# T5-bias attention and a mixture of adapters: tail bias in PSUM, a single value tile, work per pair, and a new head and close

## The chip, the cores and the metric

One core of a Trainium2 chip. The metric is the device time of one execution in microseconds. TensorE (PE) multiplies matrices into PSUM (8 banks), VectorE (DVE) and ScalarE (ACT) read PSUM, GpSimd (POOL) works on SBUF only, SyncE (SP) issues most DMAs. Each engine runs its instructions in program order and waits on semaphores for the others.

## The reference

Attention over 8 batches, 8 heads, 576 positions of 64, with a bias that depends on the distance of two positions (constant from distance 128 on), then for each of the 4608 rows a mixture of two out of eight adapters of rank 16:

```python
scores = scale * np.matmul(q, k.transpose(0, 1, 3, 2)) + bias
attn = np.exp(scores - max); attn = attn / (sum(attn) + 1e-09)
x = matmul(attn, v)                      # to (B * S, H * D)
logits = x @ w_gate                      # 8 experts, the two largest kept
w = softmax over the two
delta = sum over the two of w * ((x @ A[e]) @ B[e])
return x + delta
```

All inputs and the output are fp32.

## The kernel before

The kernel works on pairs of heads: 4 pairs a batch, 32 pairs. Of the 576 positions, 512 are split into four tiles (g = 0 to 3), and the last 64 of both heads share one 128-row tile, the tail (g = 4). A pair so has five slots; in each, `qk` multiplies scores into `sc` (two buffers of two PSUM banks), `expo` (L349) turns them into probabilities `p` in bf16, and `band` multiplies those near the diagonal by the exponential of the bias: tables M for g < 4, M4 for the tail's rows and columns, MHT for tail by tail (`tail_scores`, `tail_band`). Far from the diagonal the bias is constant and drops out in the division.

`transposes` brings q and k of a pair to kqT through PSUM (`kqps`), `tail_transposes` does so for a batch's tails (`tps` to `tlT`). `pv` multiplies probabilities with the values of `vn` and of the tail `vt`, each with a column of ones that gives the sum; 41 matmuls a pair go into two PSUM tiles of three and two row blocks. `recip` and `norm` then divide, once for each tile, into `x`; `mask_tail` zeroes the tail's off-diagonal halves. The mixture of a batch follows in later pairs: `m_xdma` transposes x by DMA (the last two batches by TensorE, `m_x`), `m_logits`, `m_gate`, `m_z`, `m_zT`, `m_out`; the tails of two batches are joined through the selecting matrix `sel` in `m_xtail` and `m_outt`.

k, q and v come as fp32 on SP's queue and are cast to bf16 by GpSimd; the tails come through GpSimd's converting DMAs (`load_tail`, L133). One bank-sized pool `acc` of four buffers serves kqps, tps, pv and all of the mixture.

The order on each engine is that of the program: one loop over 160 slots (`n = 5 * i + g`) calls `qk(n + 1)`, `expo(n)`, and then the other steps at slots that are written out. Every DVE instruction is recorded through a helper and so has line 82.

Of the kernel before, what the change touches and what calls it, by code (L numbers as in the profile page):

```python
# [27 lines left out]
def kernel(  # L28
# [13 lines left out]

    nc = tc.nc
# [10 lines left out]
    MW = 384  # L54
    PSUM = bass.MemoryType.PSUM
# [6 lines left out]
    pp = ctx.enter_context(tc.tile_pool(name="probs", bufs=2))  # L62
    xp = ctx.enter_context(tc.tile_pool(name="x", bufs=2))
    sp = ctx.enter_context(tc.tile_pool(name="small", bufs=3))
    op = ctx.enter_context(tc.tile_pool(name="outs", bufs=3))
    scp = ctx.enter_context(tc.tile_pool(name="sc_ps", bufs=2, space=PSUM))
    acp = ctx.enter_context(tc.tile_pool(name="acc_ps", bufs=4, space=PSUM))

    ident = cp.tile([128, 128], BF16, tag="ident")
    make_identity(nc, ident)  # L70
# [23 lines left out]


    kfs, vns, vfs = {}, [], {}

    def alloc_loads(b):
        kf = ldp.tile([128, H, 4 * D], FP32, name="kf", tag="kf")
        qf = ldp.tile([128, H, 4 * D], FP32, name="qf", tag="qf")  # L100
        kfs[b] = (kf, qf)
        vfs[b] = ldp.tile([128, 4, H, D], FP32, name="vf", tag="vf")

    def load_kq(b, h0, h1):
        for t, src in zip(kfs[b], (k, q)):
            nc.sync.dma_start(
                out=t[:, h0:h1, :],
                in_=src[b, h0:h1, :S4, :].rearrange("h (p j) d -> p h (j d)", j=4))

    def load_v(b, js, eng=None):  # L110
        vr = v[b, :, :S4, :].rearrange("h (t p j) d -> j t p h d", t=4, j=4)
        for j in js:
            for t in range(4):
                (eng or nc.sync).dma_start(out=vfs[b][j * 32:(j + 1) * 32, t, :, :],
                                           in_=vr[j, t])

    tls, vts = [], []
    for i in range(2):  # L120
        tl = cp.tile([128, 2, HP, 128], BF16, name=f"tl{i}", tag=f"tl{i}")
        tls.append(tl)
        vt = cp.tile([128, HP, 2 * D1], BF16, name=f"vt{i}", tag=f"vt{i}")
        vts.append(vt)
        vn = cp.tile([128, 4, H, D1], BF16, name=f"vn{i}", tag=f"vn{i}")
        vns.append(vn)

    def load_tail(b, w, e):
        sr = (k, q, v)[w][b, :, S4:, :].rearrange("(c e) p d -> e p c d", e=2)
        s = slice(e * 64, (e + 1) * 64)  # L130
        o = (tls[b % 2][s, w, :, s] if w < 2 else
             vts[b % 2][s, :, e * D1:e * D1 + D])
        nc.gpsimd.dma_start(out=o, in_=sr[e])  # L133
# [3 lines left out]
    def cast_kq(i, w, eng=None):  # L137
        b, hp = divmod(i, HP)
        if w == 0:
            kqn[i] = knp.tile([128, 2, 4, 2, D], BF16, name="kqn", tag="kqn")  # L140
        o = kqn[i][:, w].rearrange("p j h d -> p h j d")
        s = kfs[b][w][:, 2 * hp:2 * hp + 2, :].rearrange("p h (j d) -> p h j d", j=4)
        if eng is nc.scalar:
            for h in range(2):
                nc.scalar.copy(o[:, h], s[:, h])
        else:
            return (eng or nc.gpsimd).tensor_copy(o, s)  # L147

    def cast_v(i, eng=None):
        b, hp = divmod(i, HP)  # L150
        h = slice(2 * hp, 2 * hp + 2)
        return (eng or nc.gpsimd).tensor_copy(vns[b % 2][:, :, h, :D],  # L152
                                              vfs[b][:, :, h, :])

    alloc_loads(0)
    btT = cp.tile([H, NB], FP32, tag="btT")
    nc.sync.dma_start(out=btT, in_=bias_table.rearrange("b h -> h b"))
    load_kq(0, 0, 2)
    for t in tls[:1] + vts[:1]:
        dve.memset(t, 0.0)  # L160
    dve.memset(vns[0][:, :, :, D:D1], 1.0)
    for w in range(2):
        for e in range(2):
            load_tail(0, w, e)
    load_v(0, (0, 1))
    load_kq(0, 2, 4)
    load_v(0, (2, 3))
    load_kq(0, 4, 6)


# [22 lines left out]
    for bv, lo, hi in runs[nsm:]:  # L193
        n = hi - lo
# [4 lines left out]
    ge = cp.tile([H, 512], BF16, tag="ge")  # L199
    nc.scalar.activation(ge, g_sb, ACT.Exp)  # L200
    g_d = nc.dram_tensor("g_d", (H, 512), BF16, kind="Internal")
    nc.scalar.dma_start(out=g_d.ap(), in_=ge)
    cast_kq(0, 0, dve)
    cast_kq(0, 1, dve)
    cast_kq(1, 0, dve)
    cast_kq(1, 1, dve)
    gt = g_d.ap()

    Mr = cp.tile([128, H, MW], BF16, tag="Mr")
    MHr = cp.tile([128, HP, 192], BF16, tag="MHr")  # L210
    for h0, h1 in ((0, 2), (2, 4), (4, H)):
        for j in range(4):
            nc.sync.dma_start(
                out=Mr[j * 32:(j + 1) * 32, h0:h1, :],
                in_=bass.AP(tensor=gt.tensor, offset=gt.offset + h0 * 512 + j,
                            ap=[[4, 32], [512, h1 - h0], [1, MW]]))
        if h0 == 0:
            for e in range(2):
                nc.sync.dma_start(
                    out=MHr[e * 64:(e + 1) * 64],  # L220
                    in_=bass.AP(tensor=gt.tensor, offset=gt.offset + e * 512 + 192,
                                ap=[[1, 64], [1024, HP], [1, 192]]))
        if h0 == 2:
            load_kq(0, 6, H)

    M = cp.tile([128, H, 4, 96], BF16, tag="M")
    M4 = cp.tile([128, HP, 256], BF16, tag="M4")
    MHT = cp.tile([128, HP, 2, 64], BF16, tag="MHT")  # L230

    def at(t, off, *dims):
        return bass.AP(tensor=t.tensor, offset=t.offset + off,
                       ap=[t.ap[0]] + [list(d) for d in dims])

    def bias_pair(hp, eng):
        eng.tensor_copy(M[:, 2 * hp:2 * hp + 2],
                        at(Mr, 2 * hp * MW + MW - 1, (MW, 2), (-1, 4), (-4, 96)))
        eng.tensor_copy(
            M4[:, hp, 0:128].rearrange("p (j u) -> p j u", j=4),  # L240
            at(MHr, hp * 192 + 191, (-1, 4), (-4, 32)))
        eng.tensor_copy(
            M4[:, hp, 128:256].rearrange("p (h t) -> p h t", h=2),
            at(Mr, 2 * hp * MW + 127, (MW, 2), (-1, 64)))
        if hp == 0:
            eng.tensor_copy(MHT, at(MHr, 63, (192, HP), (0, 2), (-1, 64)))

    load_tail(0, 2, 0)
    load_tail(0, 2, 1)
    for t in tls[1:] + vts[1:]:  # L250
        nc.gpsimd.memset(t, 0.0)
    for vt in vts:
        nc.gpsimd.memset(vt[0:64, :, D:D1], 1.0)
        nc.gpsimd.memset(vt[64:128, :, 2 * D + 1:2 * D1], 1.0)
# [3 lines left out]
    mask = cp.tile([128, 2, 2], FP32, tag="mask")  # L258
    nc.gpsimd.memset(mask, 1.0)
    nc.gpsimd.memset(mask[64:128, 1, 0:1], 0.0)  # L260
    nc.gpsimd.memset(mask[0:64, 1, 1:2], 0.0)


    sel = cp.tile([128, 2, 128], BF16, tag="sel")
    nc.gpsimd.memset(sel, 0.0)
    for e in range(2):
        for hf in range(2):
            s = slice(hf * 64, (hf + 1) * 64)
            nc.gpsimd.tensor_copy(sel[s, e, e * 64:(e + 1) * 64], ident[s, s])

# [4 lines left out]
    def load_weights(c):  # L275
        if c < 4:
            nc.gpsimd.dma_start(out=Ab[:, c].rearrange("p (e r) -> p e r", e=E),
                                in_=moe_A[:, c * 128:(c + 1) * 128, :]
                                .rearrange("e d r -> d e r"))
            return  # L280
        nc.gpsimd.dma_start(out=Wb,
                            in_=moe_w_gate.rearrange("(c p) e -> p c e", p=128))
        nc.gpsimd.dma_start(out=Bb, in_=moe_B.rearrange("e r d -> (e r) d"))


    kqT, tlT, scs, probs, ptl, xs = {}, {}, {}, {}, {}, {}
    TPOS = {3: 0, 0: 1, 1: 2, 2: 3}

    def transposes(i):
        n = kqn.pop(i)  # L290
        ps = acp.tile([128, 2, S4], BF16, name="kqps", tag="acc")
        for w in range(2):
            for j in range(4):
                o = (ps[:, 0].rearrange("p (t j u) -> p t j u", t=4, j=4)[:, :, j] if w == 0 else
                     ps[:, 1, j * 128:(j + 1) * 128])
                nc.tensor.transpose(o, n[:, w, j], ident)  # L296
        t = kqp.tile([128, 2, S4], BF16, name="kqT", tag="kqT")
# [12 lines left out]
    def tail_scores(b):  # L310
        t = tlT[b]
        ps = acp.tile([128, HP, 128], FP32, name="tsc", tag="acc")
        for c in range(HP):
            nc.tensor.matmul(ps[:, c, :], lhsT=t[:, 0, c, :], rhs=t[:, 1, c, :],
                             start=True, stop=True)
        p = pp.tile([128, HP, 128], BF16, name="ptl", tag="ptl")
        nc.scalar.activation(p, ps, ACT.Exp, scale=scale)
        ptl[b] = p

    def tail_band(b):  # L320
        p = ptl[b]
        dve.tensor_tensor(p, p, MHT.rearrange("p c e t -> p c (e t)"), op=ALU.mult)

    def qk(n):
        i, g = divmod(n, 5)
# [4 lines left out]
        if g < 4:  # L330
            for h in range(2):
# [6 lines left out]
        nc.tensor.matmul(sc[:, 0:512], lhsT=tt[:, 0, hp, :], rhs=t[:, 1, :],  # L338
                         start=True, stop=True)
        for j in range(4):  # L340
            o = 512 + TPOS[j] * 128
            nc.tensor.matmul(sc[:, o:o + 128], lhsT=t[:, 0, j * 128:(j + 1) * 128],  # L342
                             rhs=tt[:, 1, hp, :], start=True, stop=True,
                             skip_group_check=True)

    def expo(n):
        i, g = divmod(n, 5)
        p = pp.tile([128, 2 * S4], BF16, name=f"p{g}", tag=f"p{g}")
        nc.scalar.activation(p, scs.pop(n), ACT.Exp, scale=scale)  # L349
        probs[(i, g)] = p  # L350

    def band(n):
        i, g = divmod(n, 5)
# [343 lines left out]
```

## Time and profile before

| | |
|---|---|
| median of 3 runs | 229.74 us (228.09, 229.74, 230.37) |
| span of the profiled execution, first to last instruction | 227.5 us; its own time is one of such runs, 0.6 to 2.9 us above the span |
| first, last of the 160 exponentials start | 13.26, 205.1 us |
| an exponential (128 x 1024) | 1.03 us, one starts 0.90 us after the other when nothing is waited for |
| GpSimd's tail DMAs | 48, 0.61 to 0.64 us of GpSimd each, 4.2 to 6.2 us to landing |
| kf, qf of a batch (1 MB each) | 6.2, 12.2 us to landing |
| DMA moved | 41.01 MB, 180 GB/s |

A page's busy share is a mean over stages; the windows give it by stage. In a row of a group, the number after the busy time is the mean duration in ns. Times in the chain of waits are start and length. Neighbouring instructions of one engine overlap, so that steps from start to start are shorter than durations.

### The profile page before, as it was taken

The page shows a single profiled execution, that of the slowest core. Times are in us where ns is not written, and L with a number is a line of the kernel's source. Part 1 is how long each engine was busy: PE and PEld are TensorE (multiplying, and loading weights), DVE is VectorE, ACT ScalarE, POOL GpSimd, SP SyncE. Part 2 cuts the span into 40 slices and gives each one's busy share as a digit, 9 for nine tenths or more (in the row PEclk, how much of TensorE's full clock was granted, in tenths as well). Part 3 has the DMA queues.
Part 4 walks back from the last instruction along what each step waited for, and adds up shares of the span by engine and source line. Part 5 has one row for each costly group of instructions (what it writes and reads, how often), then busy time and mean ns, then how long its engine had stood idle before and what let it go on. Part 6 is the DMA issues. An engine that isn't in the chain of part 4 may idle for free.

```text
span 227.5 us, 6531 instructions
## 1 busy us (share of the span) xinstructions
PE 176.7 (78%) x2501; PEld 120.0 (53%) x2512; DVE 188.7 (83%) x571; ACT 160.0 (70%) x178; POOL 101.5 (45%) x191
## 2 busy tenths in 40 slices
PE   0174942988989998897899689898996999977651
PEld 0032622665665665665666457566663767655520
DVE  7046881889998999998999798999996989999862
ACT  3057570899999987996889588998894788792000
POOL 8530393755554546453555445555553442220000
PEclk9998595899999999999999999999999799999958
DMA  6986899899989999999179999998699720222406
GB/s 134 205 183 189 264 237 116 155 276 131 171 253 250 146 233 278 206 92 247 76 194 300 179 247 321 160 174 217 168 311 162 188 96 0 95 95 49 184 0 230
DMA packets 86935, 41.01 MB, mean 180 GB/s; under 512 B 66800, under 2 KB 84344, under 8 KB 86904
## 3 DMA queue, kind: packets, MB, share of 16 engines
q1 hardware_dynamic: 69000, 38.75, 70.0%
q0 software_dynamic: 17888, 1.85, 17.6%
q8 instruction: 19, 0.31, 0.6%
q14 instruction: 12, 0.10, 0.2%
q10 hardware_dynamic: 16, 0.01, 0.0%
HBM read 29.84 MB, written 9.45 MB: 173 GB/s over the span
## 4 chain that ended last, share of the span: by engine, by line
DVE 35%; PE 31%; DMA 17%; ACT 8%; issue 4%; SPq 2%; POOL 1%; POOLq 0%; ACTq 0%; DVEq 0%
DMA tl<-in_q_dram 11%; DVE p L82 11%; PE pv L382 9%; ACT p L349 8%; PE sc L333 7%; DVE x L82 5%; DVE o L82 4%; PE kqps L296 3%; DVE kqT L82 3%; DVE rc L82 2%; DMA qf<-in_q_dram 2%; PE sc L338 2%; PE zp L513 2%; PE sc L342 2%; DMA g_d<-ge 2%
## 5 line engine op out<-in xcount | busy, mean ns | idle before, releaser
L349 ACT ACTIVATE p<-sc 128x1024 bf16<-128x1024 f32 x160 | 153.3, 1034 | 33.2 <-PE sc L333 14.1
L82 DVE TENSOR_TENSOR p<-p,M 128x512 bf16<-128x512 bf16 (+2 forms) x192 | 76.3, 423 | 0.0
L333 PE MATMUL sc<-kqT 64*128 64x512 bf16 x256 | 51.6, 403 | 17.3 <-ACT p L349 8.7
L382 PE MATMUL pv<-vn,p 128*128 128x65 bf16 (+1 forms) x1152 | 61.6, 200 | 0.0
L382 PEld LDWEIGHTS <-p 128*128 128x128 bf16 x1280 | 52.5, 100 | 11.7 <-issue 10.4
L147 POOL CAST kqn<-qf 128x512 bf16<-128x512 f32 x29 | 18.0, 620 | 38.8 <-DVE rc L82 38.7
L152 POOL CAST vn<-vf 128x512 bf16<-128x512 f32 x28 | 17.3, 619 | 29.9 <-DVE p L82 21.4
L333 PEld LDWEIGHTS <-kqT 64*128 64x128 bf16 x256 | 13.5, 94 | 32.4 <-issue 18.1
L382 PE MATMUL pv<-vt,p 128*128 128x130 bf16 x128 | 28.6, 223 | 0.0
L296 PE MATMUL kqps<-ident,kqn 128*128 128x128 bf16 x256 | 21.3, 229 | 8.9 <-DVE kqn L82 8.1
L296 PEld LDWEIGHTS <-kqn 128*128 128x128 bf16 x256 | 15.3, 102 | 17.8 <-DVE kqn L82 8.4
L82 DVE COPY kqT<-kqps 128x1024 bf16<-128x1024 bf16 x32 | 21.8, 682 | 2.2 <-PE kqps L296 2.1
L82 DVE TENSOR_TENSOR o<-dl,x 128x512 f32<-128x512 f32 x32 | 21.4, 680 | 0.9 <-PE dl L534 0.9
L147 POOL CAST kqn<-kf 128x512 bf16<-128x512 f32 x29 | 17.8, 614 | 9.5 <-DVE p L82 6.6
L82 DVE TENSOR_TENSOR x<-pv,rc 128x384 bf16<-128x384 f32 x32 | 17.8, 557 | 1.3 <-DVE rc L82 0.2
L82 DVE RECIPROCAL rc<-pv 128x6 f32<-128x6 f32 x64 | 11.7, 183 | 5.4 <-PE pv L382 5.1
L305 PE MATMUL tps<-ident,tl 128*128 128x128 bf16 x64 | 6.4, 236 | 11.3 <-DMA tl<-in_q_dram 11.3
L342 PEld LDWEIGHTS <-kqT 128*128 128x128 bf16 x128 | 10.6, 104 | 8.1 <-issue 2.8
L82 DVE COPY tlT<-tps 128x1024 bf16<-128x1024 bf16 x8 | 5.5, 688 | 10.9 <-PE tps L305 10.9
L338 PE MATMUL sc<-kqT,tlT 128*128 128x512 bf16 x32 | 13.1, 409 | 1.4 <-ACT p L349 1.0
L82 DVE TENSOR_TENSOR x<-pv,rm 128x256 bf16<-128x256 f32 x32 | 13.4, 417 | 0.0
L342 PE MATMUL sc<-tlT,kqT 128*128 128x128 bf16 x128 | 13.3, 231 | 0.0
(78 smaller groups left out, 190.4 us busy)
## 6 DMA issues: line engine op xcount, KB each, us to landing
vf<-in_v_dram SPq DMA_DIRECT2D x128, 64.0 KB, 4.1
out_dram<-o SPq DMA_DIRECT2D x16, 512.0 KB, 3.7
kf<-in_k_dram SPq DMA_DIRECT2D x7, 1024.0 KB, 6.2
qf<-in_q_dram SPq DMA_DIRECT2D x7, 1024.0 KB, 12.2
kf<-in_k_dram SPq DMA_DIRECT2D x4, 256.0 KB, 3.0
qf<-in_q_dram SPq DMA_DIRECT2D x4, 256.0 KB, 3.9
out_dram<-ot SPq DMA_DIRECT2D x8, 128.0 KB, 2.4
tl<-in_k_dram POOLq DMA_DIRECT2D x16, 32.0 KB, 6.2
```

Of the source, the lines that this page charges most:

```text
L82: self.last = f(*a, **kw)
L147: return (eng or nc.gpsimd).tensor_copy(o, s)
L152: return (eng or nc.gpsimd).tensor_copy(vns[b % 2][:, :, h, :D], vfs[b][:, :, h, :])
L296: nc.tensor.transpose(o, n[:, w, j], ident)
L305: nc.tensor.transpose(ps[:, w, c, :], tls[b % 2][:, w, c, :], ident)
L333: nc.tensor.matmul(sc[:, h * 512:(h + 1) * 512], lhsT=t[s, 0, g * 128:(g + 1) * 128], rhs=t[s, 1, :], start=True, stop=True)
L338: nc.tensor.matmul(sc[:, 0:512], lhsT=tt[:, 0, hp, :], rhs=t[:, 1, :], start=True, stop=True)
L342: nc.tensor.matmul(sc[:, o:o + 128], lhsT=t[:, 0, j * 128:(j + 1) * 128], rhs=tt[:, 1, hp, :], start=True, stop=True, skip_group_check=True)
L349: nc.scalar.activation(p, scs.pop(n), ACT.Exp, scale=scale)
L382: nc.tensor.matmul(acc[:, k, o:o + n], lhsT=lhsT, rhs=rhs, start=start, stop=stop, skip_group_check=True)
L513: nc.tensor.matmul(zp[:, t - t0, :], lhsT=xT[:, 4 * t + c, :], rhs=Ab[:, c, :], start=(t == t0 and c == 0), stop=(c == 3), skip_group_chec ...
```

## The change

- **Tail bias.** M4, MHT and the DVE multiplications with them go. The bias, divided by the scale, is added to the scores in PSUM by matmuls with the permutations `anti` and `perm`, before the exponential: two more per pair in `qk`, one per batch in `tail_scores`.
- **Values.** `pv` has one PSUM tile of two banks per pair (a pool of its own, one buffer) and 50 matmuls of 65 columns, ordered by head and row block. The tail's rows of an even batch go to partitions 0 to 63 and those of an odd batch to 64 to 127 (by shifted columns of p4 and ptl, with zeroed margins), into a joint tile `xts` for two batches; `sel`, `mask` and `m_outt` go. One `recip` and one `norm` (two instructions) per pair.
- **x transposed** per pair on TensorE (`m_x`), for all batches; `m_xdma` goes.
- **Pools.** `acc` has two buffers instead of four, probs three instead of two, kqT three, small and outs two.
- **Tails and weights** come by SP as fp32 and are cast by GpSimd (`cast_tail`, `cast_weights`).
- **Head.** q's first loads go on ACT's queue, half of the first v on GpSimd's; the first casts go to GpSimd and ACT; pair 1's scores come before the tails of pairs 0 and 1 (`seq`).
- **Order.** A table of events with slot and priority takes the place of the written-out loop. k and q of a batch are loaded 30 and 28 slots before its first, v and tails 25 or fewer.
- **Close.** For the last batch the gates are on DVE alone, every second output row block gets x added by a matmul with the identity and is copied by ACT, and each block is stored by itself.

```diff
-    sp = ctx.enter_context(tc.tile_pool(name="small", bufs=3))
-    acp = ctx.enter_context(tc.tile_pool(name="acc_ps", bufs=4, space=PSUM))
+    sp = ctx.enter_context(tc.tile_pool(name="small", bufs=2))
+    pvp = ctx.enter_context(tc.tile_pool(name="pv_ps", bufs=1, space=PSUM))
+    acp = ctx.enter_context(tc.tile_pool(name="acc_ps", bufs=2, space=PSUM))
...
-    def load_tail(b, w, e):
-        nc.gpsimd.dma_start(out=o, in_=sr[e])
+    def load_tail(b, w, eng=None):
+        sr = (k, q, v)[w][b, :, S4:, :].rearrange("(c e) p d -> e p c d", e=2)
+        for e in range(2):
+            (eng or nc.sync).dma_start(out=tlf[b][e * 64:(e + 1) * 64, w], in_=sr[e])
+    def cast_tail(b, what, eng=None):
+        for e in range(2):
+            s = slice(e * 64, (e + 1) * 64)
+            if what == "kq":
+                (eng or nc.gpsimd).tensor_copy(
+                    tls[b % 2][s, :, :, e * 64:(e + 1) * 64], tlf[b][s, 0:2])
+            else:
+                (eng or nc.gpsimd).tensor_copy(vts[b % 2][s, :, e, :D], tlf[b][s, 2])
...
+    load_kq(0, 0, 0, 2)
+    load_kq(0, 1, 0, 2, nc.scalar)
+    nc.scalar.dma_start(out=btT, in_=bias_table.rearrange("b h -> h b"))
+    load_kq(0, 0, 2, 4)
+    load_kq(0, 1, 2, 4, nc.scalar)
+    make_identity(nc, ident)
+    load_tail(0, 0)
+    load_tail(0, 1)
+    for j in range(2):
+        load_v(0, 2 + j, eng=nc.gpsimd)
...
+    cast_kq(0, 1, nc.gpsimd)
+    cast_kq(0, 0, nc.scalar)
...
+        mm(sc[:, 0:512].rearrange("p (j q) -> p j q", j=4)[:, :, 96:128], anti,
+           RAt[:, hp], False, True)
+        mm(sc[:, 512:640], perm, RB[:, 2 * hp:2 * hp + 2], False, True)
...
+        for m in range(m0, m1):
+            h, sl = PVORDER[m // 5]
+            g = m % 5
...
+            nc.tensor.matmul(acc[:, h, sl * D1:(sl + 1) * D1], lhsT=lhsT, rhs=rhs,
+                             start=(sl == 0 and g == 0), stop=(sl == 4 and g == 4),
+                             skip_group_check=True)
...
+    def m_x(i):
+        b, c = divmod(i, HP)
+        if c == 0:
+            xTs[b] = xp.tile([128, 4, 5, 128], BF16, name="xT", tag="xT")
+        ps = acp.tile([128, 4, 128], BF16, name="xps", tag="acc")
+        for t in range(4):
+            nc.tensor.transpose(ps[:, t, :], xs[b][:, t, 2 * c:2 * c + 2, :], ident)
+        dve.tensor_copy(xTs[b][:, c, 0:4, :], ps)
...
+    for i in range(NPAIR):
+        if i < 5:
+            pv_at[i] = (11 + 4 * i, (17, 17, 16), 14 + 4 * i)
+        else:
+            pv_at[i] = (5 * (i + 1), (5, 15, 15, 15), 5 * (i + 1) + 4)
+    for i in range(NPAIR):
+        if i >= 4:
+            on(5 * (i - 3) + 4, 13, beside, cast_kq, i, 1, nc.gpsimd)
+            on(5 * (i - 2), 29, beside, cast_kq, i, 0, nc.gpsimd)
+        if i >= 3:
+            on(5 * (i - 1), 30, transposes, i)
+        if i >= 4:
+            on(5 * (i - 1) + 1, 44, beside, cast_v, i, nc.gpsimd)
...
+        on(n_out, 10, recip, i)
+        on(n_out, 14, norm, i)
+        for g in range(4):
+            if i >= 2:
+                on(5 * i + g + 1, 12, band, i, g)
+        on(n_out + 2, 45, m_x, i)
```

## The prediction

> **What bounds the kernel now.** I read the page's busy line and slices first, to see whether one engine carries the whole span.
>
> ```profile
> span 227.5 us, 6531 instructions
> PE 176.7 (78%) x2501; PEld 120.0 (53%) x2512; DVE 188.7 (83%) x571; ACT 160.0 (70%) x178; POOL 101.5 (45%) x191
> ...
> DVE  7046881889998999998999798999996989999862
> ACT  3057570899999987996889588998894788792000
> ...
> PEclk9998595899999999999999999999999799999958
> DMA  6986899899989999999179999998699720222406
> ```
>
> VectorE (DVE) is full from slice 8 to slice 37 except in a few dips; ScalarE (ACT) has holes early and at the end; DMA is nearly full as long as there are loads. So three stages are to be costed apart: a head, a steady part, a tail. The windows give them:
>
> ```profile
> 13.30:41.90 28.60, 18.23 (x167) 11.43 (x165) 16.57 (x43) 15.36 (x16) 12.23 (x20) 0.76 1.16 193
> ...
> 130.00:168.00 38.00, 34.15 (x520) 23.60 (x523) 36.59 (x115) 33.77 (x39) 20.02 (x37) 1.00 0.99 223
> ...
> 206.10:227.50 21.40, 10.13 (x124) 6.49 (x124) 13.62 (x37) 0.26 (x2) 0.80 (x3) 0.81 0.34 123
> ```
>
> The columns are PE, PEld, DVE, ACT, POOL, then clock, DMA share, GB/s. In the head every engine is half idle; in the steady stretch DVE is busy 36.6 of 38.0 us (96%), PE 90%, ACT 89%; the last 21.4 us come after the last big exponential. What leaves the head idle is in the waits and in the chain of waits:
>
> ```profile
> ACT p L349 <- PE sc L333: 14.1, 11, 7.6
> PE tps L305 <- DMA tl<-in_q_dram: 11.3, 4, 6.3
> DVE tlT L82 <- PE tps L305: 10.9, 6, 5.8
> ```
>
> ```profile
> 29.80 8.34 DMA tl<-in_q_dram
> ...
> 98.95 5.05 DMA tl<-in_q_dram
> ...
> 122.36 5.62 DMA tl<-in_q_dram
> ...
> 168.64 5.99 DMA tl<-in_q_dram
> ```
>
> Four times PE stands in front of tps (the transposes of the tails) until GpSimd's converting DMA has landed, and everything in PE's order stands behind it. The first exponential starts at 13.26 us, after DVE had put four kqn casts ahead of the first kqT copy (11.88 us).
>
> I count in slots, one exponential each (160). Back to back they start 0.90 us apart, so a pair of heads costs ACT 4.5 us, plus a share of ptl (0.60 us per batch) and ex (0.24): 4.7. From pair 8 (66.1 us) to the last exponential's end (206.1 us) a pair takes (206.1-66.1)/24 = 5.83 us. Pairs 14, 18 and 26, with the three later tail waits, last 6.7, 7.3 and 9.1 us; against 5.4 that is 6.9 us lost, and (140.0-6.9)/24 = 5.55 us is left per undisturbed pair.
>
> **DVE per pair.** Durations overlap: the chain gives kqT and o 0.60 us each where their rows say 682 and 680 ns, so I take 80 ns off a row's mean. Now: bands 2 x 0.48 + 2 x 0.36, M4 bands 2 x 0.19, kqT 0.60, two reciprocals 0.37 (not shortened, the next waits), rm 0.08, two norms 0.48 + 0.34 = 3.93. Mixture per batch: lg 0.18, MAX8 0.34, mk 0.11, reduce and reciprocal 0.36, zt 0.71, zT 0.37, four o 2.40, half an ot 0.30, half an xtail 0.30, tlT 0.61, ptl band 0.34 = 6.0, per pair 1.5. Sum 5.43, 98% of 5.55: DVE is the bound.
>
> After: out go both M4 bands (0.38), one reciprocal (0.18), rm (0.08), the ptl band and half of each xtail (0.5 per batch). The norm becomes one of 512 elements (nearest row zt<-zp of 512 elements from PSUM, 0.61) and one of 128 on 64 partitions (zt of 128: 0.20): 0.81, nothing gained. In comes a bf16 xT copy of 512 per pair (zT row 414 ns: 0.33). So 1.68 + 0.60 + 0.19 + 0.81 + 0.33 = 3.61, mixture 5.5/4 = 1.38: 4.99. In the last 26.6 pairs seven mixtures run (b=6 is squeezed in), 1.45 per pair: 5.06; at 98% it is 5.16.
>
> **PE per pair.** Busy 90% of 5.55 is 5.0, an upper reading since ends are modelled. In: two bias matmuls (128 columns, L342 and its neighbours step 0.056) 0.11, four x transposes 0.22, pv 50 matmuls for 41. The 18 of the chain take 0.71 (0.039 each); if all 50 did, 1.97 against 0.71 + 0.41 + 0.61 = 1.73 now, +0.24; but the nine that now do 130 columns step 0.056 and become 65-wide at 0.032, which gives -0.1. Out: the sel matmuls of ot and half the xtail, 0.1. Sum 5.1 to 5.45. PE is close behind DVE, so I take 5.25 per pair, not 5.16.
>
> PE's clock was granted 1.00 from 41.9 to 168 us, with PE idle a tenth of that time, and half only after the long tail waits; kqps, half of it written to PSUM in strides, has 229 ns a matmul against 231 for contiguous L342. So I charge neither a slower clock nor the one strided bias matmul. Two rules of the Trainium skill speak against that. TensorE: Matmul & The Clock Gate, section "A second HAM failure mode: psum-queue depth-cycling", warns that micro-idling between PSUM groups makes the clock swing to half, and this change cuts the shared pool from four banks to two; if that held half of the time, PE would need about 7.6 us per pair and the run 264 us. PSUM — Partial Sum Buffer, section "Specifications (TRN2)", says that a non-contiguous pattern slows matmuls; if it doubled that one, 1.5 us in all.
>
> **GpSimd and SP.** POOL loses six tail DMAs per batch (L133 rows, 0.61 to 0.64 us each: 3.8 us) and gains four cast_tail pieces; these are not in the trace, bounds 0.26 (sel copy of 64x64) and 0.89 (768 wide), I take 0.6: 2.4 per batch. Nothing gained or lost; POOL is near half busy. The six tails go to SP as plain loads; the nearest row, vf with 64 KB, lands in 4.1 us, and the first cast comes 7 slots (6.3 us) after the issue, so the landing hides, with 2 us to spare; without it, 5 us at a batch's first tail. On SP they stand among vf, kf, qf and the outputs, which wait for DVE's o; SP issues about 26 per batch at 0.45, 12 of 21 us. The DMA transpose (six, 5.8 us) leaves, and the software queue's 17.6% of 16 engines with it: loads get freer.
>
> **Head, to slot 27** (there are 133 slots after it). Now slot 27 starts at 53.4 us. After: kf's first piece is issued 0.5 us earlier; q's cast stands on POOL behind eight software DMAs (8 x 0.62 from 1.3): cast at 6.5 to 7.1, kqT 8.2, first exponential 9.0 instead of 13.3. Pairs 1 and 2 go ahead without bands (three p buffers). Then POOL, in order, waits for batch 1's qf before cast_v(1). That load follows 2 MB of k and q, 1 MB of v, the tails and 0.7 MB of bands, with kf of batch 1 another 2 MB: 6.1 MB at the 164 to 270 GB/s of the first windows, 23 to 37 us; near 230 it is about 27. Behind it POOL has 11 casts and two M tables (0.6 and 0.89 each), 8 us, before cast_v(3); SP's next vf load waits for that, then weights (0.9 issue, 2.5 landing), then Ab and pair 6's casts and transposes: 27 + 8 + 1.9 + 3.4 + 1.8 = 42, and slot 27 at about 43 (39 to 50).
>
> **Tail.** Now lg starts 8.8 us after the last exponential, zt ends 3.4 us later, outputs end at 223.4 and 4.1 us of DMA and closing follow. After: pv 2.0, reciprocal 0.3, norms 0.9, transposes and copy 0.75, xtail 0.4, logits 0.7 = 5.0 to lg; without GpSimd in the gates 0.8 less (its waits were 0.77 and 0.43); outputs shared with ACT 1 us less: 15.8, say 16 (14.5 to 18).
>
> **Sum.** 43 + 133/5 x 5.25 = 139.7, + 16 = 198.7 us of span against 227.5. The median stands 2.2 us above the span (229.74; the runs lie 0.6 to 2.9 above it): 201 us. Of the 29 us, 10 come from the head, 13 from the steady part (7 of it tail waits), 5 from the tail.
>
> **The rivals.** *PE becomes the bound* (15%): 5.45 per pair at 98% is 5.56, +8.2: 209 us. For it: PE at 90% already; against: ends are modelled. *Loads stay late* (10%), so the change doesn't do what it says: batch 1's qf lands at 35.8 us as now, and SP's tails wait behind outputs as GpSimd's did: slot 27 at 51 or 7 us of waits back, 206 to 210 us. For it: DMA share 0.9 in the head; against: transposes and the software queue are gone. *ACT becomes the bound* (8%): 4.75 per pair, 43 + 126.4 + 16 + 2.2 = 188. Against: DVE's 4.99. *Two PSUM banks chain PE to DVE* (10%, the other side): kqps, xps and each dl share two banks, about 4.3 tiles per pair, one pv tile serves all pairs, and in the pair's last slot DVE has reciprocal, band, two norms and an o (1.95 us) in 0.9 us. If each tile held PE, and behind it the next scores, for 0.3 us, a pair takes 5.25 + 1.3 = 6.55: 43 + 174 + 16 + 2.2 = 235. It decides from 6.33 us a pair ((227.5-43-16)/26.6). Against: PE has a slot between pv's end and the next pair's pv, and the dl whose bank xps takes was written two slots earlier.
>
> **How the numbers follow.** The forecast has 55%, with 5.05 to 5.45 per pair and slot 27 at 41 to 46: 193 to 209. The rivals have 15, 10, 8 and 10%, and 2% lies between. About 1% is what a measurement of this kernel can tell from no change: faster by more 0.87, within 0.03, slower 0.10. The range for 8 in 10 reaches to PE as bound with a late head, 214, and down near ACT's case, 191.
>
> **What would show it.** Right: no wait of tps for a DMA after 50 us; first exponential near 9 us; slot 27 near 43; DVE 95% busy and 5.1 to 5.4 us a pair between 60 and 180; lg about 5 us after the last exponential. Wrong: PE waiting on DVE's o or kqT copies before kqps, xps or dl (two banks); PE busier than DVE (PE bound); clock below 1.00 in the steady part; GpSimd's q cast waiting past 33 us.

## The result and the profile after

The changed kernel takes 249.36 us (median of 4, 247.9 to 249.9) against 228.92 (227.7 to 230.4) on the same chip: 1.089 times as long, 95% interval 1.081 to 1.096. The forecast was 201 us, range 191 to 214. The profiled execution took 249.87 us, its span is 247.9. In the experiments a run more than 1.5% above the fastest of its kernel counts as slow: the times given are medians of all runs, the ratios compare the others alone with the kernel before on the same chip, so that e9's 236.0 us (two of its four runs are slow) stands beside 1.016 to 1.027.

The page's span, busy line and slices:

```profile
span 247.9 us, 7339 instructions
...
PE 193.5 (78%) x2946; PEld 134.2 (54%) x2946; DVE 179.5 (72%) x455; ACT 164.3 (66%) x182; POOL 95.9 (39%) x181
...
DVE  2715518665269979797989797979898888888561
...
PEclk9999996799859999999999999999999999999655
DMA  6956998974598439944794699547946202122206
```

DVE fell from 83 to 72% of a longer span and its row has no long full stretch any more. PE's matmuls stay at 78%, ACT and POOL fell: the page shows no new bound. The windows by stage (PE, PEld, DVE, ACT, POOL, clock, DMA share, GB/s) say more:

```profile
11.70:35.00 23.30, 16.77 (x132) 8.78 (x129) 8.55 (x15) 15.01 (x17) 5.15 (x9) 1.00 0.87 200
35.00:59.40 24.40, 15.92 (x235) 11.22 (x235) 14.45 (x31) 12.29 (x14) 11.59 (x18) 0.86 0.83 175
...
80.90:129.80 48.90, 43.89 (x737) 31.53 (x736) 42.21 (x107) 39.90 (x45) 21.70 (x38) 1.00 0.72 188
...
228.00:247.90 19.90, 10.59 (x114) 7.14 (x114) 9.93 (x30) 1.41 (x3) 0.00 (x0) 0.57 0.32 117
```

The third is eight pairs (slots 40 to 80): PE busy 43.9 of 48.9 us, 90%, DVE 86%, ACT 82%. Where the time went follows from the starts of the exponentials:

| | before | after | forecast |
|---|---|---|---|
| slot 27 starts | 53.4 us | 59.4 | 43 |
| slot 27 to slot 40 | 12.7 | 21.5 | 13.7 |
| slot 40 to the last exponential's end (24 pairs) | 140.0 | 147.1 | 126.0 |
| after it | 21.4 | 19.9 | 16 |
| span | 227.5 | 247.9 | 198.7 |

Against before, 14.8 us are lost up to slot 40 and 7.1 in the steady part, 1.5 gained at the end. Against the forecast 49.2 are missing: 24.2 up to slot 40, 21.1 in the steady part, 3.9 at the end.

The waits of the first 62 us (us in all, times, longest) show what stands in the head:

```profile
ACT p L387 <- PE sc L362: 15.7, 9, 6.0
...
POOL vn L155 <- DMA Af<-in_moe_A_dram: 7.6, 1, 7.6
DVE p L83 <- POOL M L306: 6.6, 1, 6.6
...
PE tps L332 <- POOL tl L161: 5.6, 1, 5.6
...
POOL kqn L150 <- DMA qf<-in_q_dram: 4.4, 1, 4.4
```

Batch 1's q lands at 35.6 us (35.8 before); until then 7.0 MB were moved, at 198 GB/s:

```profile
0.00:35.60 35.60, 18.60 (x142) 9.74 (x142) 15.18 (x42) 18.23 (x21) 15.73 (x40) 1.00 0.89 198
```

GpSimd stands in front of its cast, and behind it, in program order, stand a value cast, batch 1's tails and the M tables that DVE, PE and so ACT wait for. Later GpSimd stands 7.6 us before the cast of v for pair 4, until 52.9 us; the profile names a weights' load there, but the cast reads v, whose last piece lands at 52.5 us (43.5 before), behind 2 MB of batch 2's k and q.

In the waits from slot 40 to the last exponential no row of PE, DVE or ACT is for a load (GpSimd has 2.4 us before casts of v), and two rows of ACT stand out:

```profile
ACT ptl L346 <- PE tsc L343: 7.2, 6, 1.2
...
ACT ex L500 <- POOL df L494: 6.0, 6, 1.1
...
PE pv L423 <- DVE xt L83: 2.8, 7, 0.6
...
PE kqps L323 <- DVE zt L83: 2.3, 3, 0.8
```

Once per batch ACT stands before the small exponential of the tail scores, once before that of the gates, with the next large one behind it. These waits are longer than before, but not new; in the kernel before, between 66 and 206 us, they were

```profile
ACT ptl L317 <- PE tsc L314: 4.8, 6, 0.9
...
ACT ex L488 <- POOL df L477: 4.3, 5, 1.3
```

The single value tile (pv waits for xt) and the two shared banks (kqps waits for zt) cost little. The chain of waits between 121 and 126 us (start, length) shows whose work is in line there:

```profile
121.43 0.56 PE pv L423 x15
122.00 0.56 PE sc L369 x7
...
122.60 1.00 ACT p L387
...
123.65 0.39 PE sc L362 x2
124.04 1.00 PE zp L525 x16
125.04 0.32 PE sc L362 x2
125.36 0.55 PE kqps L323 x8
```

Scores have two buffers, so PE may be one slot ahead of ACT and no more. A slot with 15 pv and 7 tail scores takes PE 1.12 us, more than ACT's 0.90, and the chain runs on PE. At 122.60 it passes to ACT, which had stood 1.06 us before ex until 122.45; PE waits 0.64 us for this large exponential to give a score buffer free. Then two score matmuls and z make a slot of 1.39.

### The profile page after: what moved, and what is told of

It is laid out like the page before. It is cut to its first block, busy times and chain, and to the rows that moved or that the text cites. A ratio compares the mean times of both kernels' runs of the same rounds, so it can differ in the third digit from the quotient of the medians.

```text
span 247.9 us, 7339 instructions
## 1 busy us (share of the span) xinstructions
PE 193.5 (78%) x2946; PEld 134.2 (54%) x2946; DVE 179.5 (72%) x455; ACT 164.3 (66%) x182; POOL 95.9 (39%) x181
## 4 chain that ended last, share of the span: by engine, by line
PE 51%; DVE 13%; DMA 12%; SPq 10%; ACT 7%; issue 4%; POOL 1%; ACTq 0%; DVEq 0%
PE pv L423 18%; PE sc L362 11%; PE sc L369 5%; ACT pt L387 5%; PE kqps L323 4%; DMA vf<-in_v_dram 3%; SPq L125 3%; PE zp L525 3%; DMA tlf<-in_q_dram 3%; PE xps L463 3%; SPq L119 3%; DVE x L83 2%; DMA Mr<-g_d 2%; PE dl L548 2%; DMA btT<-in_bias_table_dram 2%
## 5 line engine op out<-in xcount | busy, mean ns | idle before, releaser
L387 ACT ACTIVATE p<-sc 128x1024 bf16<-128x1024 f32 x128 | 125.8, 1029 | 30.1 <-PE sc L362 29.1
L83 DVE TENSOR_TENSOR p<-p,M 128x512 bf16<-128x512 bf16 (+1 forms) x128 | 66.6, 527 | 8.5 <-POOL M L306 6.6
L423 PE MATMUL pv<-vn,p 128*128 128x65 bf16 x1024 | 58.8, 198 | 7.3 <-DVE xt L83 7.3
L423 PE MATMUL pv<-vt,pt 128*128 128x65 bf16 x256 | 45.6, 198 | 0.0
L423 PEld LDWEIGHTS <-pt 128*128 128x128 bf16 x512 | 35.2, 100 | 6.8 <-issue 6.8
L387 ACT ACTIVATE pt<-sc 128x1024 bf16<-128x1024 f32 x32 | 32.7, 1020 | 8.2 <-PE sc L369 8.1
L83 DVE TENSOR_TENSOR x<-pv,rc 128x512 bf16<-128x512 f32 x32 | 21.9, 683 | 0.1
L83 DVE COPY xT<-xps 128x512 bf16<-128x512 bf16 x32 | 13.5, 422 | 9.5 <-PE xps L463 9.1
L423 PE MATMUL pv<-vn,pt 128*128 128x65 bf16 x256 | 19.1, 198 | 0.0
L548 PE MATMUL dl<-Bb,zT 128*128 128x512 bf16 x36 | 14.6, 415 | 0.8 <-DVE zT L83 0.6
```

The source lines that it names most:

```text
L83: self.last = f(*a, **kw)
L387: nc.scalar.activation(p[:, 0:2 * S4], scs.pop(n), ACT.Exp, scale=scale)
L423: nc.tensor.matmul(acc[:, h, sl * D1:(sl + 1) * D1], lhsT=lhsT, rhs=rhs, start=(sl == 0 and g == 0), stop=(sl == 4 and g == 4), skip_group ...
L548: nc.tensor.matmul(ps, lhsT=zT[:, t, :], rhs=Bb, start=True, stop=eng is None, skip_group_check=True)
```

## Experiments

The theories, numbered as the expectations name them: 1, GpSimd's program order holds the head; 2, the loads come too late, by their bytes or by their place on the queues; 3, ACT's program order (small exponentials waiting) costs the steady part; 4, PE is full, or too full in single slots; 5, the single value tile holds PE. DVE as bound is the prediction's own reading.

| run | time, us | ratio to before, 95% | slot 27 | slot 40 | slots 40 to 80 |
|---|---|---|---|---|---|
| changed kernel | 249.4 | 1.081 to 1.096 | 59.4 | 80.9 | 49.0 |
| e1_pool_order | 243.9 | 1.066 to 1.077 | 52.3 | 76.0 | 49.0 |
| e2_load_order | 246.4 | 1.075 to 1.084 | 56.3 | 77.3 | 48.8 |
| e3_act_order | 245.4 | 1.070 to 1.081 | 58.8 | 81.2 | 47.8 |
| e4_pv_split | 246.5 | 1.072 to 1.084 | 58.5 | 78.2 | 49.1 |
| e5_act_later | 238.1 | 1.031 to 1.052 | 60.5 | 77.8 | 45.9 |
| e6_dve_less | 245.6 | 1.065 to 1.086 | 59.8 | 81.3 | 48.4 |
| e7_pe_less | 241.8 | 1.049 to 1.069 | 58.5 | 79.1 | 47.5 |
| e8_head | 247.4 | 1.074 to 1.090 | 51.2 | 80.7 | 48.8 |
| e9_fill | 236.0 | 1.016 to 1.027 | | | |
| e10_head2 | 236.4 | 1.026 to 1.036 | 60.2 | 77.1 | 45.9 |
| e11_all | 235.9 | 1.019 to 1.034 | | | |
| e12_head3 | 234.4 | 1.023 to 1.031 | 58.5 | 74.8 | 45.9 |
| e13_head3_fill | 232.0 | 1.013 to 1.021 | 58.5 | 73.6 | 43.8 |
| e14_fill_xdma | 247.3 | (242.4 to 251.6 us) | 59.3 | 78.8 | 46.7 |
| e15_head4_fill | 235.0 | 1.008 to 1.030 | 52.3 | 75.6 | 43.5 |
| e16_head4_weights | 232.1 | 1.013 to 1.024 | 54.4 | 74.3 | 43.9 |
| e17_v_first | 234.9 | 1.024 to 1.034 | 52.5 | 75.9 | 43.8 |
| e18_pool_late | 230.8 | 1.006 to 1.016 | 53.1 | 71.9 | 43.3 |

**e1_pool_order**: GpSimd's casts of batch 1, the tails' and the weights' moved behind what pairs 1 to 3 need.

```diff
-            on(5 * (i - 3) + 4, 13, beside, cast_kq, i, 1, nc.gpsimd)
+            on({4: 15, 5: 17}.get(i, 5 * (i - 3) + 4), 35 if i < 6 else 13,
+               beside, cast_kq, i, 1, nc.gpsimd)
...
-        on(5 * (p - 4) + 4 if nb > 1 else 12, 62, cast_tail, nb, "kq")
+        on(5 * (p - 4) + 4 if nb > 1 else 17, 62, cast_tail, nb, "kq")
-    on(19, 60, cast_weights, 0)
+    on(30, 60, cast_weights, 0)
```

> The changed kernel with another order of GpSimd's early work only: the casts of pairs 4 and 5 (batch 1, whose loads land at 35.6 us) and the cast of batch 1's tails come after the casts and tables of pairs 1 to 3; pair 4's transposes and batch 1's tail transposes come at slots 18 and 20 instead of 15 and 14; the weights' casts come at slots 27 and 30. Theory 1 (GpSimd's program order: one cast that waits for a load holds eight others, and PE behind them): the waits of ACT from 36 to 42 us (6.05) and of DVE for M (6.6) go, pair 8 starts at 70 to 75 us instead of 80.9, the run takes 239 to 243 us instead of 249. Theory 2 (the loads themselves are too slow): the same load is waited for one step later, pair 8 starts at 78 or later, 246 to 250 us. The steady period (49.0 us per eight pairs) stays in both.

The waits at 36 to 42 us go and slot 27 comes 7.1 us earlier, but 6.3 us stand after pair 5 instead; at slot 40 4.9 us are left, and the run, 243.9 us, lies between the two expectations. For scale: e6 and e7 below, whose edits start after slot 40, have slot 27 at 59.8 and 58.5 and slot 40 at 81.3 and 79.1, so that 2 us there are no finding.

**e2_load_order**: batch 2's k and q (2 MB) at slots 19 and 21 instead of 10 and 12.

```diff
-        on(at_k, 60, load_kq, nb, 0, 0, H)
+        at_l = 19 if nb == 2 else at_k
+        on(at_l, 60, load_kq, nb, 0, 0, H)
```

> The changed kernel with batch 2's k and q loads issued at slots 19 and 21 instead of 10 and 12, so that batch 1's v, the weights and batch 2's tails stand ahead of them on SyncE's queue. Theory 1 (GpSimd's order alone): batch 1's q still lands at 35.6 us, the stall from 36 to 42 us stays, and only the waits near 44 to 53 us (7.56 before pair 4's v cast) shrink: pair 8 at 75 to 79 us, 243 to 247 us. Theory 2 (loads too slow, in the wrong order): 2 MB less ahead of what is needed, pair 8 at 70 to 74, 238 to 242 us. If later pairs wait for batch 2's k and q instead, no gain: 249 us.

Slots 27 and 40 come 3.1 and 3.6 us earlier, as theory 1 had allowed (slot 40 at 75 to 79, the run at 243 to 247): the place on the queue counts too, but by less than theory 2 had put it at.

**e3_act_order**: the tail scores before pv in their slot, all gates on DVE.

```diff
-        on(5 * p + 3, 50, tail_scores, nb)
+        on(5 * p + 3, 35, tail_scores, nb)
-            on(n + at_[1 + part], 51, m_gate, b, part, late)
+            on(n + at_[1 + part], 51, m_gate, b, part, True)
```

> The changed kernel with two things done earlier so that ScalarE does not stand before them in its order: the tail-by-tail scores come ahead of that slot's pv on PE (ptl waited 7.2 us in six batches of the steady part), and the gates of all batches are on VectorE (ex waited 6.0 us for GpSimd's df). Theory 3 (ScalarE's program order: small instructions that wait hold the next big exponential): 1.2 us per batch each, ACT's idle time before ptl and ex goes, the period of eight pairs falls from 49.0 to 44.5 to 46 us, the run to 237 to 241 us. Theory 4 (PE is full, 4.5 us of matmul steps and about 1 us of changes between 64-row and 128-row tiles per pair): PE's wait for ACT shrinks but the period stays above 48 us, 246 to 249 us.

Eight pairs lose 1.2 us. ACT's wait before ptl falls from 7.2 to 4.1 us; that before ex stays (6.8, now for DVE's df). 47.8 us miss both expectations (44.5 to 46, above 48). A weak form of the test, which e5 repeats.

**e4_pv_split**: two one-bank value tiles, divided one after the other.

```diff
-            pvs[i] = pvp.tile([128, 2, 512], FP32, name="pv", tag="pv")
+            pvs[i] = [pvp.tile([128, 512], FP32, name=f"pv{h}", tag=f"pv{h}") for h in range(2)]
```

> The changed kernel with the value tile as two tiles of one bank, one per head, and a reciprocal and norms for each head, the first a slot earlier: same banks, same matmuls. Theory 5 (the single value tile: pv of a pair waits for the norm of the pair before): PE's waits for xt (5.9 us in all in the head, 1.6 and part of 3.6 later) go, 242 to 246 us. Theory 4 or 3: the waits of pv for xt go but the time stays, or DVE's additional reciprocal and two short norms (0.35 us per pair) show where DVE is late: 248 to 253 us.

Eight pairs stay at 49.1 us, though pv's wait for xt between slot 40 and the last exponential falls from 2.8 to 0.3 us. Theory 5 falls for the steady part, and with it the part of the rival "two PSUM banks" that lies in the value tile. The two shared banks were left as they are in all runs; against them speak only kqps' 2.3 us of waiting.

**e5_act_later**: both small exponentials one slot after what feeds them.

```diff
+        on(5 * p + 4, 5, tail_exp, nb)
...
-        for part in range(4):
-            on(n + at_[1 + part], 51, m_gate, b, part, late)
+        for part in (0, 4, 1, 2, 3):
+            x = at_[1] + (b < B - 2) if part == 4 else at_[1 + part]
+            on(n + x, 50 if part == 4 and b < B - 2 else 51, m_gate, b, part, late)
```

> The exponential of a batch's tail by tail scores (ptl) and the one of the gates (ex) are written one slot later than the matmuls and the subtraction that feed them, for all batches but the last two in the case of the gates, so that ScalarE finds them ready. Nothing else changes. In the changed kernel ScalarE's order costs a gap of about 1.8 us at ptl and about 0.8 us at ex per batch, beyond a usual slot. Theory 3 (small ScalarE instructions stand in front of the large exponentials and wait): eight pairs take 49.0 - 2 x 2.6 = 44 to 46 us, the run ends near 239 us. Theory 4 (PE is full, ScalarE's stalls are only where PE's shortage shows): eight pairs stay at 48 to 49 us, the run near 246 to 249.

45.9 us for eight pairs, no wait of ptl or ex left in them, 11 us of time: theory 3 is shown. As the kernel before has such waits too, the same edit might help it; that was not run. Between slots 40 and 80 the same PE work now fills 94% of the window:

```profile
77.80:123.60 45.80, 43.19 (x734) 31.31 (x736) 42.51 (x107) 40.20 (x45) 21.57 (x38) 1.00 0.75 198
```

**e6_dve_less** and **e7_pe_less** each take work from one engine alone.

```diff
-            if i >= 2:
+            if 2 <= i < 8 or i >= 8 and g in (0, 3):
                 on(5 * i + g + 1, 12, band, i, g)
```

> Leaves out part of the computation: from pair 8 on the two middle bands (g = 1 and 2) are not multiplied on VectorE. That is about 0.9 us of VectorE per pair and nothing of PE, ScalarE or GpSimd. If VectorE is the bound of the steady part, eight pairs take 49.0 - 7 = 42 us, and the run loses 20 us or more. If VectorE is only late where others make it late (theories 3 and 4), eight pairs take 47.5 to 49 us and the run loses under 5.

```diff
             g = m % 5
+            if g == 1 and i >= 8:
+                continue
```

> Leaves out part of the computation: from pair 8 on the ten pv matmuls of the values' second tile (g = 1) are not done. That is 10 x 0.029 = 0.29 us of PE per pair, spread over its four slots with pv, and nothing of the others. Theory 4 (PE's program order is the bound): eight pairs lose 8 x 0.29 = 2.3 us, 49.0 to 46.7, and the run 6 to 7 us. Theory 3 (ScalarE's order): less than half of that. VectorE as bound: nothing.

Their windows over slots 40 to 80:

```profile
81.30:129.70 48.40, 43.33 (x734) 31.56 (x737) 34.58 (x92) 40.04 (x46) 20.05 (x38) 1.00 0.71 188
```

```profile
79.10:126.60 47.50, 41.07 (x664) 29.51 (x667) 42.13 (x106) 39.82 (x46) 21.37 (x38) 1.00 0.74 194
```

DVE loses 7.6 us of work (42.2 to 34.6) and the window only 0.6: DVE is not the bound of this kernel. PE loses 2.8 (43.9 to 41.1) and the window 1.5, between what theories 3 and 4 gave: PE's order is on the path. ACT's waits before ptl and ex are nearly as long as ever there (2.1 us each; 2.4 and 2.1 in the changed kernel), which would explain the rest; that is not shown.

**e9_fill**: e5 with PE's work spread over the slots.

```diff
-        at_ = ((4, 7, 8, 9, 9, 8, 9, 12, 14, 17, 19, 22) if b < B - 2 else
+        at_ = ((4, 7, 8, 9, 9, 8, 14, 22, 25, 27, 32, 37) if b < B - 3 else
...
+            on(n + at_[6], 52, m_z, b, 0, 2)
+            on(n + at_[6] + 5, 52, m_z, b, 2, tiles(b))
...
-        on(5 * (p - 3) + 3 if nb > 1 else 14, 50, tail_transposes, nb)
+        on(5 * (p - 2) + 4 if nb > 1 else 14, 50, tail_transposes, nb)
```

> On top of e5_act_later: for batches 0 to 4 the z matmuls are split in two halves, each in the last slot of a pair (which has only two score matmuls and at most one dl), the tail transposes move into such a slot too, and the dl matmuls go one by one to slots with little else. The same work, spread over the slots. In e5_act_later a batch still has z in one slot, which leaves 1.35 and then 2.04 us between exponentials in every eight pairs, and tps beside 22 matmuls. Theory 4 (PE can be only one slot ahead of ScalarE, so a slot with too much costs its excess and a light one gives nothing back): eight pairs from 45.9 to 43 to 44 us (the sum of PE's slots, 21.4 us per batch, sets the floor of 42.8), the run 5 to 8 us below e5_act_later's 238.1. If PE's total alone counts, or another engine sets 45.9: 45 to 46, the run the same.

The steady part is read from e13_head3_fill, which has the same one; slots 40 to 80 and 80 to 120:

```profile
73.60:117.40 43.80, 43.26 (x739) 30.69 (x737) 40.95 (x105) 40.24 (x46) 21.13 (x38) 1.00 0.73 192
117.40:162.40 45.00, 43.95 (x739) 30.88 (x737) 42.50 (x109) 40.37 (x46) 21.36 (x37) 1.00 0.77 199
```

Eight pairs take 43.8 us, as theory 4 had it (43 to 44). PE is busy 98.8% of the first window with the same matmuls as before the edit: with even slots it is PE's sum that fills them, 5.4 to 5.6 us a pair. The run gained less than the 5 to 8 us expected (e13, with the edit, is 2.4 us below e12, without it), since work put off to later slots makes the last 40 longer: 49.1 us with 44.9 of PE, against 46.6 with 42.6 in e12_head3. Over all 120 slots of the steady part that leaves 0.5 us.

**e14_fill_xdma**: e9 with x of batches 0 to 4 transposed by DMA.

```diff
+        if b < B - 3:
+            if c == HP - 1:
+                nc.sync.dma_start_transpose(
+                    out=xTs[b][:, 0:16], in_=xs[b].rearrange("p t h d -> p (t h d)"))
+            return
```

> On top of e9_fill: x of batches 0 to 4 is transposed by DMA once per batch, as in the kernel before, in place of four PE transposes and a VectorE copy per pair; the mixture of these batches comes five slots later, so that the transfer is not waited for. PE loses per pair 0.22 us and a change of operand of about 0.1 us, VectorE 0.33 us. If PE's work is the floor of e9_fill: pairs 8 to 23 go from 89 us to 84 to 85.5, the run 4 to 6 us below e9_fill's 236. If not, 88 to 90, or more if the transfers delay the loads.

As a whole a miss: pairs 8 to 23 took 95.5 us and the run 247.3. Six undisturbed pairs (9 to 14), in two windows, are as expected:

```profile
85.20:100.14 14.94, 14.94 (x269) 10.86 (x266) 13.07 (x37) 14.31 (x18) 8.82 (x15) 1.00 0.96 229
100.14:115.61 15.47, 15.47 (x269) 11.09 (x267) 14.13 (x34) 14.64 (x17) 8.82 (x14) 1.00 0.76 176
```

PE is busy without a gap at 5.07 us a pair, where e13 takes 5.43 for the same six: 0.36 less for about 0.32 of PE work taken out. The edit takes as much from DVE, and e6 ruled DVE out only in the changed kernel; that PE and not DVE is the floor here rests on PE's 100% beside DVE's 87 and 91%. But at pairs 7, 15, 19 and 23 an exponential starts 2.9 to 6.1 us after the one before, by these waits (60 to 180 us):

```profile
POOL vn L155 <- DMA vf<-in_v_dram: 15.7, 4, 5.8
...
ACT ex L515 <- POOL df L507: 15.0, 5, 5.0
```

With the DMA transposes v comes late, GpSimd stands before its cast, and the gate behind it holds ACT. The work is paid on one side or the other.

**The head.** e8_head joins e1, e2 and the bias table first on ACT's queue:

```diff
+    nc.scalar.dma_start(out=btT, in_=bias_table.rearrange("b h -> h b"))
     load_kq(0, 0, 0, 2)
     load_kq(0, 1, 0, 2, nc.scalar)
-    nc.scalar.dma_start(out=btT, in_=bias_table.rearrange("b h -> h b"))
```

> Three edits of the head together: GpSimd's early order and the transposes behind it as in e1_pool_order, batch 2's k and q loaded at slots 19 and 21 as in e2_load_order, and the bias table first on ScalarE's DMA queue. One by one the first two gave 5.4 and 2.9 us of time. The bias table's landing moves from 6.3 to about 3 us, and the tables made from it by as much. If the late start is a sum of these (theories 1 and 2): slot 40 at 81 - 4.9 - 3.6 - 2 = 70 to 72 us, the run near 238 to 240. If one of them only hides the other (the loads as a whole are too slow): slot 40 at 75 to 77, the run near 243. The steady part stays at 49.0 us for eight pairs in both.

The first exponential comes at 9.4 us instead of 11.7 (in e2, e4 and e9, with the bias table still third, it came at 9.5, so the edit need not be the cause) and slot 27 at 51.2, but slot 40 at 80.7: batch 2's k now stands on SP behind the weights, batch 2's tails and part of its v, and lands at 61.5 us. A miss for both theories as stated.

e10_head2 and e12_head3 (both on e5, e1's order and the bias table first) move batch 1's k and q up, the first on SP ahead of v's tails, the second to ACT's queue at 7 us:

```diff
+    alloc_loads(1)
+    load_kq(1, 0, 0, H)
+    load_kq(1, 1, 0, H)
     load_tail(0, 2)
```

> On top of e5_act_later: GpSimd's early order as in e1_pool_order, the bias table first on ScalarE's queue, and on SP the bias tables' loads before the second half of v, and batch 1's k and q before the tails of v and out of the loop. Theory 2 (the early loads come late because of where they stand on SP's queue): RA lands at 15 to 17 us instead of 21 to 22, batch 1's q at 28 to 31 instead of 35, slot 27 starts at 44 to 47 (60.5 in e5_act_later), slot 40 at 68 to 71 (77.8), the run at 228 to 232. If the loads are late because 16 DMA engines are full with 6 MB whatever their order: slot 27 at 51 to 53, slot 40 at 75 or later, the run at 234 to 238.

```diff
     nc.scalar.dma_start(out=g_d.ap(), in_=gx)
+    alloc_loads(1)
+    load_kq(1, 0, 0, H, nc.scalar)
+    load_kq(1, 1, 0, H, nc.scalar)
```

> On top of e5_act_later: GpSimd's early order and the bias table first, as in e10_head2; in its place on the queues, batch 1's k and q are issued by ScalarE right after the tables' write (near 7 us), and on SP the tails of v, the last k and q of batch 0 and a quarter of v stand ahead of the tables, another quarter behind them. In e10_head2 the tails of v stood behind 2 MB of batch 1 and held pv of pair 0 for 10 us at slot 12, and SP idled from 6.3 to 13.2 us behind the tables' write. Theory 2 (place on the queues): batch 1's k and q land at 22 to 26 us, slot 27 starts at 46 to 50, slot 40 at 66 to 70 (77 in e10_head2), the run at 225 to 229. If the bytes set it: slot 40 at 74 or later, the run at 234 to 237.

Each made one new wait. In e10 between 15 and 45 us pv of pair 0 stands behind v's tails, which now land behind 2 MB:

```profile
POOL vt L164 <- DMA tlf<-in_v_dram: 9.4, 1, 9.4
...
PE pv L431 <- POOL vt L164: 5.6, 1, 5.6
```

In e12 it was the tables (RA at 27.2 us, 5.1 us of PE before tsc) and ACT's own issues (first exponential 13.0). Slot 40 at 77.1 and 74.8 is in both where it was expected if the bytes set it. e11_all is e10 with e9's steady part, e13_head3_fill e12 with it:

> e9_fill and e10_head2 together. If both work and add up: 221 to 226 us, below the kernel before; if only the steady part or only the head works: 228 to 233; if neither: near e5_act_later's 238.

> e12_head3 with the steady part of e9_fill (1.5 to 2.5 us less than e5_act_later's). If theory 2 holds, 222 to 227 us, ahead of the kernel before; if not, 232 to 236.

Neither fits what was said if both parts work: e11 took 235.9 us, e13 232.0.

e15 to e18 go step by step, each moving what the last had left waiting: tails and the last k and q into SP's idle time; weights and batch 2's tails before its v; batch 1's v before batch 2's k and q; at last GpSimd's casts alone.

```diff
+    load_tail(0, 2)
+    load_kq(0, 0, 6, H)
+    load_kq(0, 1, 6, H)
     Mr = cp.tile([128, H, MW], BF16, tag="Mr")
```

> e11_all with another order on SP's queue: tails of v and last k and q of batch 0 before the tables, then v's second half, the other bands, and batch 1's k and q last. Theory 2 (place on the queues): the 10 us stall at slot 12 goes and no other takes its place: slot 15 at 31 to 33 (42.1 in e11_all), slot 27 at 49 to 53, slot 40 at 68 to 71 (78.0), the run at 225 to 229. If the bytes set it, the time goes into later waits and slot 40 stays at 74 or later, the run at 231 to 235.

```diff
-        on(14 + c, 60, load_weights, c)
+        on(12, 59, load_weights, (c + 4) % 5)
-        at_t = 5 * (p - 5) + 2 if nb > 1 else 8
+        at_t = (5 * (p - 5) + 2 if nb > 2 else 13) if nb > 1 else 8
```

> e15_head4_fill with the five loads of the weights at slot 12 and batch 2's tails at slot 13, ahead of batch 2's v (slot 15 on). Theory 2 (place on the queues): the 7 us at slot 30 fall to 1 to 2, slot 40 starts at 69 to 71 us (75.6), the run at 227 to 231. If the loads as a whole are late: another of them holds the same stretch, slot 40 at 74 or later, the run at 233 to 236.

```diff
-        at_k = 5 * (p - 6) if nb > 1 else 6
+        at_k = (5 * (p - 6) if nb > 2 else 13) if nb > 1 else 6
```

> e16_head4_weights with batch 2's k and q issued together at slot 13, behind all of batch 1's v and the weights, as the kernel before orders them. Theory 2 (place on the queues): batch 1's v is complete at 42 to 45 us (62), batch 2's k and q land at 54 to 60, slot 27 starts at 49 to 52 (54.4), slot 40 at 66 to 70 (74.3), the run at 223 to 228, level with the kernel before or below it. If the loads as a whole are late: slot 40 at 73 or later with the wait at batch 2's k and q instead, the run at 230 to 234.

```diff
-        on(5 * (p - 4) + 4 if nb > 1 else 17, 62, cast_tail, nb, "kq")
+        on((33 if nb == 2 else 5 * (p - 4) + 4) if nb > 1 else 17, 62, cast_tail, nb, "kq")
```

> e17_v_first with GpSimd's casts of batch 2's tails moved from slots 24 and 27 to 33 and 38 and of its first q and k from 29 and 30 to 33 and 34, behind the casts of the weights and the first gate. Theory 1 (GpSimd's program order): the 7.8 us at slot 30 fall under 2.5, slot 40 starts at 67 to 71 us (75.9), the run at 226 to 231. If the loads themselves hold it: the time comes back at slots 33 to 36 as a wait for batch 2's tails, k or q, slot 40 at 74 or later, the run at 233 to 236.

e15 brought slot 27 to 52.3 us, then 7.0 us stood after slot 30; e16 took these away and 5.1 came after slot 28; e17 had batch 1's v complete at 45.6 us (near 56 in e16; the 62 of its expectation was a piece of batch 2) and 7.8 after slot 30, with this in its waits from 52 to 66 us:

```profile
POOL tl L161 <- DMA tlf<-in_q_dram: 9.2, 1, 9.2
...
PE lp L487 <- POOL Wb L302: 6.1, 1, 6.1
```

GpSimd stood before tails that nobody needed yet, with the gate weights, which PE needed, behind them. e18, which moved only GpSimd's casts, took slot 30's gap to 1.3 us and slot 40 to 71.9; 2 to 3 us came back at pair 7. For the place on the queues e15, e16 and e17 are misses: slot 40 stayed at 74.3 to 75.9 us, where it was put for the case that the loads as a whole are late, and only e18 came near its forecast. Theories 1 and 2 can't be parted by these runs: a late load costs what stands behind its cast on GpSimd, and a reordered cast only moves the cost if its load is late. That the bytes themselves hold the head is not ruled out. e18 is 18.6 us below the changed kernel and still 1.1% above the one before (1.006 to 1.016); a version faster than before was not found.

## Why the prediction was wrong, point by point

- **"At 98%: DVE is the bound"**, then 5.25 us a pair: this step failed. A pair took 6.13, and 6.12 in slots 40 to 120. There, of the 0.87 us over, e5 returns 0.38 (ACT's small exponentials), even slots 0.19 (5.55 in e13), and 0.30 is what stays above 5.25, with PE busy nearly all the time. In slots 120 to 160 evening out costs most of what it had gained. The sum per engine was made as if each could work ahead; with two score buffers and written-out program order each slot takes its own longest engine.
- **PE, "5.1 to 5.45"**: busy went from 5.09 (40.7 us in slots 40 to 80 of before) to 5.49 a pair, just over the range; the pair's time in these slots went up by as much, from 5.73 to 6.12. The rival "PE becomes the bound" had the right engine and nearly the right floor, but no price for uneven slots: it gave 209 us.
- **ACT**: ptl and ex were charged their durations, 0.60 and 0.24 us. In order on ACT they cost their waits too, 1.2 and about 1.0 us per batch, which the sum put at nothing although the profile of before has 0.8 and 0.9 for each such wait. No rival had this.
- **DVE per pair, 4.99 to 5.16**: measured 5.28 (42.2 us in slots 40 to 80), only 0.09 less than the 5.36 of before in the same slots. Bands of 768 elements have 604 ns instead of 554; why is not known. By e6 it is no matter for the time of the changed kernel.
- **Slot 27 at 43 us**: failed. "About 27" for batch 1's q was 35.6, the time of the rival "Loads stay late", which priced slot 27 at 51: the sum had 6.1 MB ahead of it at 230 GB/s, and 7.0 MB were moved by then at 198. The waits in GpSimd's order behind it and the next loads behind those (v at 52.5, the first weights' cast at 56.7) make 59.4, and slot 40 lost 7.8 more (the last weights' casts at 62 and 63.3, with batch 2's tails behind them). e18, with e5's and e9's edits in it, gets 9.0 of the 24.2 us missing up to slot 40 back; what holds the rest stays open. First exponential 11.7 instead of 9.0: on ACT the table's exponential waits 4.8 us for the bias table, third on its queue. With that order the first exponential came at 9.5 to 11.7 us in ten profiled runs, with the table first (e8, e10, e11, e15 to e18) at 9.1 to 9.6.
- **Tail 16 us**: 19.9. lg starts 7.2 us after the last exponential, not 5.0: the last pair's pv waits 2.0 us for the norm of the pair before it, since there is one value tile, a term that the sum put at nothing, and takes 2.6 us, not 2.0 (clock granted 0.57 there). From lg on, 8.6 us of work and 4.1 of landing and closing were as before; the 1.8 us that were to be saved there did not come.
- **Right**: tps waits once more for the tails after 50 us, 3.2 us for GpSimd's cast of batch 2's before slot 40, and no more after 82 us (four times before, with 25.0 us of DMA in its chain); cast_tail at 0.6 us (0.61 and 0.39); the strided bias matmul (runs of 32 columns) has 225 ns beside 223 for its neighbour, so the slowdown that PSUM — Partial Sum Buffer, "Specifications (TRN2)", warns of is not seen; the clock was granted 1.00 from 81 to 228 us, so with two shared banks the swing of "A second HAM failure mode: psum-queue depth-cycling" (TensorE: Matmul & The Clock Gate) is not seen either.
- **Two PSUM banks, 235 us**, the rival on the slower side: not what happened. kqps before zt is 2.3 us, pv before xt 2.8 in 147 us, and e4, which frees pv, changed nothing in the steady part.

## What to carry to other kernels

Where program order is written out and an engine can be only one slot ahead of another, add up each slot's longest engine rather than each engine's total, and read the chain of waits for whose work stands in line: an engine that is busy 90% of the time can already hold the path where its slots have no slack. A small instruction on a busy engine costs the wait for its input and what stands behind it (ptl and ex here 2.2 us of waiting a batch), so put it one slot later than its producer. Before moving loads to a queue, list what is issued ahead of each and what stands behind each cast: in the head nearly every reordering here uncovered the next wait.

## What had not been expected of the hardware

SP's issue instructions, 0.3 to 0.6 us as a rule, stretch to 2.0 to 4.4 us when loads of 1 MB are in flight ahead of them (2.7 and 4.4 us for the first tail load behind batch 1's k and q in the changed kernel and in e16), and small loads then land 5 to 9 us after issue (5.7 and 9.2 in the changed kernel) against about 2 us with little in flight (Mr in e10: 1.8 to 2.0). PE's busy row can reach 100% of a window (15.47 of 15.47 us in e14) with the clock at 1.00; since the ends of matmuls are modelled, that does not say that no work could be added.
